# Attention and two gated MLPs on one core: clears, scaling, a mean, a sum and a weight-decoding step stand elsewhere in the order

## The chip, the core and the metric

The kernel runs on one core of a Trainium2 chip. The core has four engines that compute: PE (TensorE, matrix products and transposes), DVE (VectorE), ACT (ScalarE) and POOL (GpSimd). SP (SyncE) issues most of the transfers. Each engine works through its own queue in order; engines wait for one another through semaphores. The metric is the device time of one execution in microseconds (us), lower is better, as the median of three runs.

## What is computed

```python
q_n, k_n = rmsnorm(q, g_q), rmsnorm(k, g_k)          # q, k, v: (4, 12, 448, 64)
scores = (1 / sqrt(64)) * q_n @ k_n.T                # per batch and head
scores = scores - max(scores, axis=-1)
attn = exp(scores)
attn = attn / (sum(attn, axis=-1) + 1e-9)
x = (attn @ v) as (1792, 768)                        # 4*448 tokens, 12*64 features
x = (x @ w_a) * (x @ w_b) @ w_out                    # 768 -> 1536 -> 768
x = sigmoid(x @ w_gate) * (x @ w_val) @ w_out2
```

All of it is fp32. The kernel splits every operand of a large product into a high and a low part and adds three products.

## The kernel before

The work has two stages. **Attention** takes 24 items, an item being two heads of one batch. **The two MLPs** follow as one long stream of matrix products (lines 1026, 1313 and 1323), with weights that are decoded, split and stored on the way.

The order of the attention stage is written out by hand. Four tables hold steps such as `(s, 0, 1)`: `begin` is run once, `first` is the turn for item 1, `turns` is run for each of items 2 to 22, and `end` finishes the last two items and starts the MLPs. In `first` and `turns` the second entry is an offset: in one turn the scores of item i are made, the output of item i-1 is formed, item i-2 is normalised and stored, and items i+1 to i+4 are prepared. What a step issues is put on the engines' queues in the table's order, so the table sets the order on each engine.

The steps that matter here, with their lines:

- `load`, `load_r`, `load_g`: transfers of q, k, the last 64 rows of each head, and the gains g. `load_g` issues its four small transfers from POOL's queue (lines 193, 194); the others come from SP.
- `squares`, `mean` or `sums`, `rsqrt`, `newton`: the factor 1/rms of an item. `mean` (line 251) and `newton` (273 to 275) are on DVE, `rsqrt` (265, 266) on ACT, `squares` of most items on POOL (227 to 229).
- `scale`: q (part 0), k (part 1) and the 64 remaining rows (part 2) times that factor; on DVE for item 0, on POOL for the others (284, 297). `gain` (244) makes the vector G of both gains.
- `t_tr`: PE transposes of the scaled k (part 1) or q (part 0). `k_hi` (339, ACT) and `k_lo` (350, DVE) make the two parts of k, times G; `q_hi` and `q_lo` (334) those of q. The first of k's transposes reads a block that holds the last slot of q and the remaining rows of k.
- `s` (371, PE): scores. `top` (377, DVE): minus their row maximum, nm. `exp` (390, ACT): exponentials P, with row sums. Each item has seven of them; `top` and `exp` of parts 0 and 4 come first in a turn.
- `x_tr` (153, PE) and `x_out` (424 on ACT, 422 on DVE) turn P into pt; `pv` (436, PE) multiplies it with v.
- `rsum` (443, 444, DVE): 1/(sum + 1e-9) of the item before; `rsum_tr`, `rsum_post`, `rsum_get` bring it into rows by PE, ACT and SP; `norm` (473, DVE) multiplies two turns' old output with it; `put` stores.
- `decode(i, 0)` and `decode(i, 1)`: each one step of preparing MLP weights, taken from a generator: it may give DVE one of the lines 721, 723, 727 or 654, ACT one of 720 or 840, a load, or nothing.
- `early_hi` and `early_lo` (499 on ACT, 505 on POOL) split finished outputs in turns 15 to 20. `warm` (533) are transposes on PE whose result nobody reads.

Ahead of `begin` stand memsets: on POOL the identity's, then the tails of three P buffers (line 144), two rs buffers (147) and two rz buffers (156). DVE clears pv and others.

```python
        def rsum(i):
            d = st[i]
            rc = sm.tile([P, 7], F32, tag="rc", name="rc")
            nc.vector.tensor_scalar_add(rc, d["sum"], 1e-9)
            nc.vector.reciprocal(out=rc, in_=rc)
            d["rc"] = rc
```

Of the kernel before, what the change touches and what calls it, by code (L numbers as in the profile page):

```python
# [10 lines left out]
F32 = mybir.dt.float32  # L11
# [3 lines left out]
ALU = mybir.AluOpType  # L15
# [8 lines left out]
def attention_then_two_gated_mlps(  # L24
# [37 lines left out]
    nc = tc.nc  # L62
    B, H, S, D = q.shape
    NT, DM = out.shape
    DFF = moe_w_a.shape[1]
    P = 128
# [48 lines left out]
    def attention():  # L115
        actx = ExitStack()
        pr = actx.enter_context(tc.tile_pool(name="pr", bufs=2))
        sm = actx.enter_context(tc.tile_pool(name="sm", bufs=3))
# [23 lines left out]
        P3 = [fx.tile([P, 512], F32, name=f"P3{i}") for i in range(3)]  # L142
        for t in P3:
            nc.gpsimd.memset(t[:, S:512], 0.0)
        rs = [fx.tile([P, 512], F32, name=f"rs{i}") for i in range(2)]
        for t in rs:
            nc.gpsimd.memset(t, 0.0)
        pvs = ps_v.tile([P, 512], F32, tag="pv", name="pv")
        nc.vector.memset(pvs, 0.0)

        def turned(out, in_, b):
            w = out.shape[-1]
            nc.tensor.transpose(out, in_[rows[b]], ident[rows[b], rows[b]])  # L153
# [8 lines left out]
        st = [dict() for _ in range(NPAIR)]  # L162
# [263 lines left out]
        def pv(i, j):  # L426
# [3 lines left out]
            for h in range(2):  # L430
# [7 lines left out]
                )  # L438

        def rsum(i):  # L440
            d = st[i]
            rc = sm.tile([P, 7], F32, tag="rc", name="rc")
            nc.vector.tensor_scalar_add(rc, d["sum"], 1e-9)
            nc.vector.reciprocal(out=rc, in_=rc)
            d["rc"] = rc

# [83 lines left out]
        def warm(i, n):  # L530
# [4 lines left out]
        begin = (  # L535
            (warm, 0, 26), (load, 0), (load_r0, 0), (load, 1), (load_g, 0), (load_r, -4), (load_r, -3), (load_r, -6),
            (load_r, -5), (load, 2), (load_r, -2), (load_r, -1), (load_v, 0), (squares, 0),
            (sums, 0, (7, 13), (0, 7), (13, 14)), (rsqrt, 0), (squares, 1), (newton, 0),
            (scale, 0, 1), (scale, 0, 2), (gain, 0), (scale, 0, 0), (load, 3), (load_r, 0), (load_v, 1), (load_r, 1),
            (t_tr, 0, 1), (warm, 0, 4), (k_hi, 0), (t_tr, 0, 0), (warm, 0, 6), (sums, 1, (7, 13)), (k_lo, 0), (q_hi, 0),  # L540
# [8 lines left out]

        first = (  # L550
            (mean, 2), (s, 0, 0), (rsqrt, 2), (rsum, -1), (t_tr, 1, 1), (top, 0, 0), (k_hi, 1), (exp, 0, 0), (x_tr, -1, 0), (top, 0, 4),
            (k_lo, 1), (x_out, -1, 0, 0), (s, 0, 1), (x_out, -1, 0, 1), (newton, 2), (exp, 0, 4),
            (x_tr, -1, 1), (x_out, -1, 1, 0), (load, 4), (load_r, 3), (load_v, 1), (t_tr, 1, 0), (rsum_tr, -1), (rsum_post, -1),
            (pv, -1, 0), (scale, 2, 2), (x_out, -1, 1, 1), (top, 0, 1), (q_hi, 1), (scale, 2, 1), (exp, 0, 1), (pv, -1, 1),
            (x_tr, -1, 2), (top, 0, 5), (q_lo, 1), (x_out, -1, 2, 0), (s, 0, 2), (x_tr, -1, 3),
# [3 lines left out]

        turns = (  # L560
            (early, 0), (early_hi, -1), (squares, 3), (early_lo, -1), (decode, 0, 0), (s, 0, 0), (rsum, -1), (t_tr, 1, 1),
            (top, 0, 0), (k_hi, 1), (exp, 0, 0), (x_tr, -1, 0), (top, 0, 4), (k_lo, 1), (x_out, -1, 0, 0), (s, 0, 1),
            (x_out, -1, 0, 1), (norm, -2), (mean, 3), (exp, 0, 4), (x_tr, -1, 1), (x_out, -1, 1, 0),
            (load, 4), (load_r, 3), (load_v, 1), (t_tr, 1, 0), (rsum_tr, -1), (rsum_post, -1), (put, -2),
# [5 lines left out]

        end = (
            (close, -1), (s3, -1, fetch_third, 0), (s, -1, 0), (x_tr, -2, 0), (rsum, -2), (top, -1, 0),
            (exp, -1, 0), (x_out, -2, 0, 0), (top, -1, 4), (x_out, -2, 0, 1), (exp, -1, 4), (norm, -3), (put, -3),
            (x_tr, -2, 1), (s, -1, 1), (x_out, -2, 1, 0), (x_out, -2, 1, 1), (rsum_tr, -2), (rsum_post, -2), (top, -1, 1),
# [3 lines left out]
            (decode, -1, 0), (decode, -1, 1), (x_tr, -1, 0),  # L578
            (close_s, -1), (rsum, -1), (x_out, -1, 0, 0), (decode, -1, 2), (x_out, -1, 0, 1), (x_tr, -1, 1), (rsum_tr, -1), (norm, -2),
            (rsum_post, -1), (put, -2), (x_out, -1, 1, 0), (decode, -1, 3), (x_out, -1, 1, 1), (decode, -1, 4),  # L580
# [821 lines left out]
    with tc.manual_schedule():  # L1402
        main = mlps()
        attention()
        open_places(6, 4, 2, 3)
        begin_mm("mm1", 3)
        for c in range(KC):
            place(where[0]["A22"], "l", c, F32, "f")
        for n, c in (("A22", 0), ("A21", 0), ("A22", 1), ("A21", 1), ("A21", 2), ("A22", 2)):
            stage_in(0, n, c)  # L1410
        for c in range(KC):
            stage_in(0, "A11", c)
        low_third(1)
        sum_third(2)
        next(main)
        cast_third(2)
        next(main)
        next(main)
        low_third(2)
        ready[0] = True  # L1420
        for _ in main:
            pass
# [29 lines left out]
```

## Time and profile before

| | |
|---|---|
| median of three runs | 1211.89 us (1210.01 to 1212.42) |
| the profiled execution's own time | 1213.13 us |
| its span on the core | 1211.4 us |
| PE busy | 1164.7 us, 96% |
| DVE busy | 930.9 us, 77% |
| ACT busy | 666.5 us, 55% |
| POOL busy | 157.3 us, 13% |
| mean granted clock of PE | 0.989 |

The span is read in two parts. Up to about 283 us the four engines share the attention stage, and each of them waits for others; from there PE works without a pause to the end. POOL works in the first part only. Shares over the whole span therefore say little about either part; the stages are read one by one. All times below are from the span's start. "Granted clock" is the share of full speed that PE was given: 1.00 is 2.4 GHz, 0.50 is 1.2 GHz.

### The profile page before, as it was taken

To read this page: it belongs to the slowest core of one execution; us is meant where nothing else is said; L and a number is where in the kernel's file an instruction comes from. 1 tells how busy PE (TensorE), PEld (TensorE's weight loads), DVE (VectorE), ACT (ScalarE), POOL (GpSimd) and SP (SyncE) were. 2 spreads that over 40 slices of the span, in tenths; PEclk is the share of its full clock that TensorE was granted. 3 is DMA by queue.
4 is the path that set the end of the run, shared out by engine and by line. 5 is a ranking of instruction groups with operands and counts; after the bars stand their busy time and mean duration, and the time that the engine had idled before them with its cause. 6 is when DMAs were issued, how large, how long until landed. Compare 5 with 4: busy or idle time off the path is not lost.

```text
span 1211.4 us, 19984 instructions
## 1 busy us (share of the span) xinstructions
PE 1164.7 (96%) x7236; PEld 1009.4 (83%) x7236; DVE 930.9 (77%) x1603; ACT 666.5 (55%) x1298; POOL 157.3 (13%) x246
## 2 busy tenths in 40 slices
PE   6888888999999999999999999999999999999998
PEld 5555554557999999999999999899999999999998
DVE  6899999977868677875768688976776877667673
ACT  5787888974633443444455566544545344445542
POOL 4665577710000000000000000000000000000000
PEclk8999999999999999999999999999999999999999
DMA  5344454439245565654865753234655654777682
GB/s 134 106 132 118 138 155 143 124 107 329 69 134 171 135 210 154 190 185 130 303 232 170 252 168 115 96 110 133 192 188 143 205 169 144 243 274 243 189 272 94
DMA packets 144370, 205.88 MB, mean 170 GB/s; under 512 B 24808, under 2 KB 118160, under 8 KB 144272
## 3 DMA queue, kind: packets, MB, share of 16 engines
q1 hardware_dynamic: 143712, 204.18, 53.9%
q8 instruction: 57, 0.93, 0.3%
q10 hardware_dynamic: 432, 0.43, 0.1%
q14 instruction: 41, 0.34, 0.1%
q0 software_dynamic: 128, 0.00, 0.0%
HBM read 150.21 MB, written 54.35 MB: 169 GB/s over the span
## 4 chain that ended last, share of the span: by engine, by line
PE 82%; DVE 8%; ACT 7%; issue 1%; DMA 1%; POOL 1%; SPq 0%; DVEq 0%; ACTq 0%; POOLq 0%
PE mm L1026 49%; PE mm L1313 13%; PE mm L1323 12%; PE pv L436 4%; ACT P L390 3%; PE s L371 3%; DVE nm L377 2%; ACT pt L424 2%; PE tr L153 2%; DVE pt L422 1%; DVE y L275 1%; DVE xl L654 1%; ACT KH L339 1%; DVE d L727 0%; DMA qk<-in_q_dram 0%
## 5 line engine op out<-in xcount | busy, mean ns | idle before, releaser
L1026 PE MATMUL mm<-xh,wh 128*128 128x448 f32 x1008 | 369.6, 367 | 0.7 <-ACT u L1078 0.4
L1026 PE MATMUL mm<-xh,wl 128*128 128x448 f32 x1008 | 369.0, 366 | 0.8 <-DVE wl L654 0.8
L1026 PE MATMUL mm<-xl,wh 128*128 128x448 f32 x1008 | 368.9, 366 | 0.0
L1026 PEld LDWEIGHTS mm<-xh,wh 128*128 128x128 f32 x1008 | 189.4, 188 | 19.8 <-issue 2.6
L1026 PEld LDWEIGHTS mm<-xh,wl 128*128 128x128 f32 x1008 | 189.5, 188 | 16.9 <-DVE wl L654 1.1
L1026 PEld LDWEIGHTS mm<-xl,wh 128*128 128x128 f32 x1008 | 189.5, 188 | 15.4
L654 DVE TENSOR_TENSOR wl<-d,wh 128x384 fp32r<-128x384 f32 x250 | 136.5, 552 | 66.3 <-ACT wh L1186 41.9
L840 ACT CAST wh<-d 128x384 fp32r<-128x384 f32 x166 | 81.9, 513 | 99.9 <-DVE d L828 80.2
L727 DVE SCALAR_TENSOR_TENSOR d<-d,raw 128x384 uint32<-128x384 uint32 x138 | 77.6, 562 | 53.3 <-ACT d L720 47.8
L390 ACT ACTIVATE P<-s,nm 128x448 f32<-128x448 f32 x166 | 105.3, 642 | 23.1 <-DVE nm L377 23.0
L720 ACT ACTIVATE d<-raw 128x384 f32<-128x384 f32 x138 | 75.9, 555 | 74.9 <-DMA raw<-in_moe_w_out_dram 42.3
L1186 ACT CAST wh<-d 128x384 fp32r<-128x384 f32 x84 | 43.2, 514 | 123.2 <-issue 40.4
L1323 PE MATMUL mm<-wh,gh 128*128 128x384 f32 x294 | 98.7, 336 | 0.2 <-ACT mm L1294 0.2
L1323 PE MATMUL mm<-wl,gh 128*128 128x384 f32 x294 | 98.6, 335 | 0.0
L1323 PE MATMUL mm<-wh,gl 128*128 128x384 f32 x294 | 98.5, 335 | 0.0
L377 DVE TENSOR_REDUCE nm<-s 128x1 f32<-128x448 f32 x166 | 94.0, 612 | 3.3 <-PE s L371 2.6
L1313 PE MATMUL mm<-gh,wl 128*128 128x448 f32 x252 | 92.0, 365 | 0.0
L1313 PE MATMUL mm<-gh,wh 128*128 128x448 f32 x252 | 92.0, 365 | 0.0
L1313 PE MATMUL mm<-gl,wh 128*128 128x448 f32 x252 | 92.0, 365 | 0.0
L371 PE MATMUL s<-KH,QH 64*128 64x448 f32 (+1 forms) x166 | 55.9, 461 | 29.4 <-ACT P L390 29.1
L723 DVE SCALAR_TENSOR_TENSOR raw<-raw 128x384 uint32<-128x384 uint32 x140 | 79.1, 565 | 4.0
L436 PE MATMUL pv<-pt,v 128*64 128x448 f32 x288 | 73.4, 596 | 2.0 <-DVE pt L422 0.6
(162 smaller groups left out, 1924.8 us busy)
## 6 DMA issues: line engine op xcount, KB each, us to landing
gd<-u SPq DMA_DIRECT2D x60, 448.0 KB
u<-gd SPq DMA_DIRECT2D x60, 448.0 KB
d<-wd SPq DMA_DIRECT2D x132, 192.0 KB
raw<-in_moe_w_out_dram SPq DMA_DIRECT2D x48, 384.0 KB
wd<-d SPq DMA_DIRECT2D x72, 192.0 KB
raw<-in_moe_w_a_dram SPq DMA_DIRECT2D x24, 384.0 KB
raw<-in_moe_w_b_dram SPq DMA_DIRECT2D x24, 384.0 KB
raw<-in_moe_w_val_dram SPq DMA_DIRECT2D x23, 384.0 KB
```

Source lines behind the costliest of these rows:

```text
L371: nc.tensor.matmul(out_, w[e, o:o + P], x[e, m:m + S], start=(n == 0), stop=(n == 2))
L377: nc.vector.tensor_reduce(out=d["nm"][:, t:t + 1], in_=d["ps"][t], axis=AX.X, op=ALU.max, negate=True)
L390: nc.scalar.activation(out=e, in_=d["ps"].pop(t), func=AF.Exp, bias=d["nm"][:, t:t + 1], accum_out=d["sum"][:, t:t + 1])
L436: nc.tensor.matmul(pvs[64 * h:64 * h + 64, o:o + S], w, x, start=(n == 0), stop=(n == R), skip_group_check=True)
L654: eng.tensor_tensor(out=lo, in0=t, in1=f32(hi), op=ALU.subtract)
L720: nc.scalar.activation(out=f32(t), in_=f32(high), func=AF.Copy, scale=2.0 ** -112)
L723: nc.vector.scalar_tensor_tensor(out=low, in0=high, scalar=0x80000000, in1=low, op0=ALU.bitwise_and, op1=ALU.bitwise_or)
L727: nc.vector.scalar_tensor_tensor(out=t, in0=t, scalar=3, in1=low, op0=ALU.logical_shift_left, op1=ALU.bitwise_or)
L840: nc.scalar.copy(out=hi, in_=t)
L1026: nc.tensor.matmul(ps[:, o:o + S], w[:, P * c:P * c + P], x[:, x0:x0 + S], start=(p in (1, 5) and c == 0 and z == 0), stop=(c == KC - 1 an ...
L1313: nc.tensor.matmul(ps[:, o:o + S], w[:, P * un:P * un + P], g[:, g0:g0 + S], start=(p in (1, 5) and f == 0 and z == 0), stop=(f == HF - 1 ...
L1323: nc.tensor.matmul(ps[:, o:o + HB], g[:, P * t:P * t + P], w, start=(p in (1, 5) and f == 0 and z == 0), stop=(f == HF - 1 and z == 2), sk ...
```

## The change

- **Prologue.** The clears of the P tails and the rs buffers become a step `clear`, which stands in `begin` behind `load_g`. The rz buffers are still cleared ahead of it.
- **Prologue.** `scale` of item 0: q's scaling follows k's at once; the remaining rows and `gain` come after both.
- **First turn.** `mean` of item 3 (offset 2) moves from the head of `first` to behind the second `x_out`; `rsqrt`, `newton` and `scale` of that item follow later too, and k is scaled ahead of the remaining rows.
- **Sums.** The addition of 1e-9 becomes a step `total` on POOL, ahead of `rsum`. In `turns` it stands behind `squares`, at the turn's head; `rsum` keeps the reciprocal alone and moves from ahead of `top` to behind `norm`. In `first` it moves alike, to behind `mean`. In `end` both stand where `rsum` stood.
- **Decoding.** `decode(0, 0)` moves from the turn's head to behind `norm` and `rsum`.

```diff
-        for t in P3:
-            nc.gpsimd.memset(t[:, S:512], 0.0)
...
-        for t in rs:
-            nc.gpsimd.memset(t, 0.0)
...
+        def clear(i):
+            for t in P3:
+                nc.gpsimd.memset(t[:, S:512], 0.0)
+            for t in rs:
+                nc.gpsimd.memset(t, 0.0)
...
+        def total(i):
+            d = st[i]
+            d["rc"] = sm.tile([P, 7], F32, tag="rc", name="rc")
+            nc.gpsimd.tensor_scalar(out=d["rc"], in0=d["sum"], scalar1=1e-9, scalar2=None, op0=ALU.add)
+
         def rsum(i):
-            d = st[i]
-            rc = sm.tile([P, 7], F32, tag="rc", name="rc")
-            nc.vector.tensor_scalar_add(rc, d["sum"], 1e-9)
+            rc = st[i]["rc"]
             nc.vector.reciprocal(out=rc, in_=rc)
-            d["rc"] = rc
...
-            (early, 0), (early_hi, -1), (squares, 3), (early_lo, -1), (decode, 0, 0), (s, 0, 0), (rsum, -1), (t_tr, 1, 1),
+            (early, 0), (early_hi, -1), (squares, 3), (total, -1), (early_lo, -1), (s, 0, 0), (t_tr, 1, 1),
...
-            (x_out, -1, 0, 1), (norm, -2), (mean, 3), (exp, 0, 4), (x_tr, -1, 1), (x_out, -1, 1, 0),
+            (x_out, -1, 0, 1), (norm, -2), (rsum, -1), (decode, 0, 0), (mean, 3), (exp, 0, 4), (x_tr, -1, 1), (x_out, -1, 1, 0),
```

The order on PE and on SP is the same in both kernels. Three places where it differs follow; the changed kernel's line numbers are up to four higher.

POOL in the prologue, from the identity's memset to the first copy of KH; before:

```order
masks.py:197 MEMSET ident 128x128
L144 MEMSET P_280 128x64
L144 MEMSET P_281 128x64
masks.py:199 ISA
masks.py:199 AFFINE_SELECT ident<-ident 128x128
L144 MEMSET P_282 128x64
L147 MEMSET rs_286 128x512
L147 MEMSET rs_287 128x512
L156 MEMSET rz_292 128x768
L156 MEMSET rz_293 128x768
L193 DMA gg<-in_g_q_dram 64x1
L194 DMA gg<-in_g_k_dram 64x1
```

and in the changed kernel:

```order
masks.py:197 MEMSET ident 128x128
L158 MEMSET rz_287 128x768
masks.py:199 ISA
masks.py:199 AFFINE_SELECT ident<-ident 128x128
L158 MEMSET rz_288 128x768
L195 DMA gg<-in_g_q_dram 64x1
L196 DMA gg<-in_g_k_dram 64x1
L195 DMA gg<-in_g_q_dram 64x1
L196 DMA gg<-in_g_k_dram 64x1
L149 MEMSET P_280 128x64
L149 MEMSET P_281 128x64
L149 MEMSET P_282 128x64
```

Five clears went from ahead of the gain's transfers to behind them, and one clear of rz now stands ahead of the select that makes the identity.

DVE where `begin` ends and the first turn starts (the first nm is still item 0's); before:

```order
L377 TENSOR_REDUCE nm<-s 128x1
L251 TENSOR_REDUCE ms<-sq 128x14
L443 TENSOR_SCALAR rc<-sum 128x7
L444 RECIPROCAL rc<-rc 128x7
L377 TENSOR_REDUCE nm<-s 128x1 x2
L350 SCALAR_TENSOR_TENSOR KL<-tr,G,KH 128x4x64 x2
```

and in the changed kernel:

```order
L379 TENSOR_REDUCE nm<-s 128x1 x3
L352 SCALAR_TENSOR_TENSOR KL<-tr,G,KH 128x4x64 x2
L253 TENSOR_REDUCE ms<-sq 128x14
L449 RECIPROCAL rc<-rc 128x7
L424 COPY pt<-tr 128x7x64
```

The mean and the reciprocal went behind the maxima and k's low part, and the addition left the engine.

DVE from the end of turn 3 into turn 4, with one weight step at each end; before:

```order
L721 TENSOR_SCALAR raw<-raw 128x384
L273 SCALAR_TENSOR_TENSOR t<-y 128x14
L274 SCALAR_TENSOR_TENSOR t<-ms,t 128x14
L275 SCALAR_TENSOR_TENSOR y<-t,y 128x14
L723 SCALAR_TENSOR_TENSOR raw<-raw 128x384
L443 TENSOR_SCALAR rc<-sum 128x7
L444 RECIPROCAL rc<-rc 128x7
L377 TENSOR_REDUCE nm<-s 128x1 x2
L350 SCALAR_TENSOR_TENSOR KL<-tr,G,KH 128x4x64 x2
L473 TENSOR_TENSOR xs<-pv,rs_286 128x512
L251 TENSOR_REDUCE ms<-sq 128x14
L422 COPY pt<-tr 128x7x64
```

and in the changed kernel:

```order
L725 TENSOR_SCALAR raw<-raw 128x384
L275 SCALAR_TENSOR_TENSOR t<-y 128x14
L276 SCALAR_TENSOR_TENSOR t<-ms,t 128x14
L277 SCALAR_TENSOR_TENSOR y<-t,y 128x14
L379 TENSOR_REDUCE nm<-s 128x1 x2
L352 SCALAR_TENSOR_TENSOR KL<-tr,G,KH 128x4x64 x2
L477 TENSOR_TENSOR xs<-pv,rs_283 128x512
L449 RECIPROCAL rc<-rc 128x7
L727 SCALAR_TENSOR_TENSOR raw<-raw 128x384
L253 TENSOR_REDUCE ms<-sq 128x14
L424 COPY pt<-tr 128x7x64
```

The maxima now follow the Newton step directly; the reciprocal and the second weight step stand between `norm` (xs) and `mean` (ms).

## Rows read from the trace of the kernel before

**Rows 1.** Waits of PE, 285 us to the end, longest: us in total, times, longest.
```profile
PE mm L1026 <- DVE wl L654: 0.8, 1, 0.8
```

**Rows 2.** Chain of waits, 0 to 17 us: start us, us, what.
```profile
1.57 0.92 POOL rs L147 x2
...
5.55 3.69 DMA gg<-in_g_k_dram
...
13.87 1.47 PE s L371 x6
```

**Rows 3.** Timeline, prologue: start, us, engine, line, tiles, count [idle before <-releaser].
```profile
8.05 0.27 PE L153 MATMUL tr<-ident,qkn 64*128 64x64 f32 x1 [1.30 <-DVE qkn L297]
...
9.44 0.55 DVE L284 TENSOR_TENSOR qkn<-qk,y 128x384 f32<-128x384 f32 x1
...
10.77 0.69 ACT L339 ACTIVATE KH<-tr,G 128x512 fp32r<-128x512 f32 x1 [3.42 <-PE tr L153]
```

**Rows 4.** Timeline, the first turn's head, several engines.
```profile
25.14 0.47 PE L153 MATMUL tr<-ident,qkn 64*128 64x64 f32 x8 [1.02 <-POOL qkn L297]
...
26.34 1.26 DVE L443 TENSOR_SCALAR rc<-sum 128x7 f32<-128x7 f32 x1
...
28.36 0.64 ACT L390 ACTIVATE P<-s,nm 128x448 f32<-128x448 f32 x1 [0.78 <-DVE nm L377]
...
29.14 0.74 PE L371 MATMUL s<-KH,QH 64*128 64x448 f32 x1 [2.85 <-ACT P L390]
```

**Rows 5.** Timeline of ACT, `k_hi` alone: one for each turn, nine shown.
```profile
40.95 0.69 ACT L339 ACTIVATE KH<-tr,G 128x512 fp32r<-128x512 f32 x1 [0.95 <-PE tr L153]
...
92.38 0.69 ACT L339 ACTIVATE KH<-tr,G 128x512 fp32r<-128x512 f32 x1 [0.54 <-PE tr L153]
104.57 0.69 ACT L339 ACTIVATE KH<-tr,G 128x512 fp32r<-128x512 f32 x1 [0.66 <-PE tr L153]
114.94 0.69 ACT L339 ACTIVATE KH<-tr,G 128x512 fp32r<-128x512 f32 x1 [0.56 <-POOL sq L229]
127.17 0.69 ACT L339 ACTIVATE KH<-tr,G 128x512 fp32r<-128x512 f32 x1 [0.64 <-PE tr L153]
...
199.47 0.69 ACT L339 ACTIVATE KH<-tr,G 128x512 fp32r<-128x512 f32 x1
213.03 0.69 ACT L339 ACTIVATE KH<-tr,G 128x512 fp32r<-128x512 f32 x1
223.03 0.69 ACT L339 ACTIVATE KH<-tr,G 128x512 fp32r<-128x512 f32 x1
...
253.30 0.69 ACT L339 ACTIVATE KH<-tr,G 128x512 fp32r<-128x512 f32 x1 [0.91 <-PE tr L153]
```

**Rows 6.** Timeline of POOL and DVE in the turn from 61 us.
```profile
64.47 0.45 POOL L297 TENSOR_SCALAR qkn<-rqk,y 128x64 f32<-128x64 f32 x1 [3.72 <-PE tr L153]
...
64.78 0.62 DVE L422 COPY pt<-tr 128x448 f32<-128x448 f32 x1 [0.29 <-ACT pt L424]
```

**Rows 7.** Chain of waits, 58 to 125 us, at that turn's head.
```profile
60.79 0.47 DVE raw L723
61.26 0.09 DVE rc L443
...
61.37 0.20 DVE rc L444
```

**Rows 8.** Timeline, POOL and DVE at 199 us.
```profile
199.43 2.07 POOL L505 TENSOR_TENSOR xl<-xst,xh 128x896 fp32r<-128x896 f32 x1 [0.30 <-ACT xh L499]
199.47 2.07 DVE L443 TENSOR_SCALAR rc<-sum 128x7 f32<-128x7 f32 x1
```

**Rows 9.** Timeline of PE and ACT, the turn from 92 us.
```profile
91.31 0.54 ACT L840 CAST wh<-d 128x384 fp32r<-128x384 f32 x1
...
94.52 0.59 PE L371 MATMUL s<-KH,QH 64*128 64x448 f32 x1 [1.54 <-ACT P L390]
```

**Rows 10.** Windows: length, busy of PE, PEld, DVE, ACT, POOL, then PEclk, DMA, GB/s.
```profile
95.00:96.00 1.00, 1.00 (x16) 1.00 (x14) 1.00 (x3) 0.95 (x3) 0.00 (x0) 0.50 0.99 212
```

More of the change, by code (lines that the diff above doesn't have):

```diff
@@ L535, in attention @@
         begin = (
-            (warm, 0, 26), (load, 0), (load_r0, 0), (load, 1), (load_g, 0), (load_r, -4), (load_r, -3), (load_r, -6),
+            (warm, 0, 26), (load, 0), (load_r0, 0), (load, 1), (load_g, 0), (clear, 0), (load_r, -4), (load_r, -3), (load_r, -6),
             (load_r, -5), (load, 2), (load_r, -2), (load_r, -1), (load_v, 0), (squares, 0),
             (sums, 0, (7, 13), (0, 7), (13, 14)), (rsqrt, 0), (squares, 1), (newton, 0),
-            (scale, 0, 1), (scale, 0, 2), (gain, 0), (scale, 0, 0), (load, 3), (load_r, 0), (load_v, 1), (load_r, 1),
+            (scale, 0, 1), (scale, 0, 0), (scale, 0, 2), (gain, 0), (load, 3), (load_r, 0), (load_v, 1), (load_r, 1),
             (t_tr, 0, 1), (warm, 0, 4), (k_hi, 0), (t_tr, 0, 0), (warm, 0, 6), (sums, 1, (7, 13)), (k_lo, 0), (q_hi, 0),
@@ L550, in attention @@
         first = (
-            (mean, 2), (s, 0, 0), (rsqrt, 2), (rsum, -1), (t_tr, 1, 1), (top, 0, 0), (k_hi, 1), (exp, 0, 0), (x_tr, -1, 0), (top, 0, 4),
-            (k_lo, 1), (x_out, -1, 0, 0), (s, 0, 1), (x_out, -1, 0, 1), (newton, 2), (exp, 0, 4),
+            (total, -1), (s, 0, 0), (t_tr, 1, 1), (top, 0, 0), (k_hi, 1), (exp, 0, 0), (x_tr, -1, 0), (top, 0, 4),
+            (k_lo, 1), (x_out, -1, 0, 0), (s, 0, 1), (x_out, -1, 0, 1), (mean, 2), (rsum, -1), (exp, 0, 4),
             (x_tr, -1, 1), (x_out, -1, 1, 0), (load, 4), (load_r, 3), (load_v, 1), (t_tr, 1, 0), (rsum_tr, -1), (rsum_post, -1),
-            (pv, -1, 0), (scale, 2, 2), (x_out, -1, 1, 1), (top, 0, 1), (q_hi, 1), (scale, 2, 1), (exp, 0, 1), (pv, -1, 1),
+            (pv, -1, 0), (rsqrt, 2), (x_out, -1, 1, 1), (top, 0, 1), (q_hi, 1), (newton, 2), (scale, 2, 1), (scale, 2, 2), (exp, 0, 1), (pv, -1, 1),
             (x_tr, -1, 2), (top, 0, 5), (q_lo, 1), (x_out, -1, 2, 0), (s, 0, 2), (x_tr, -1, 3),
@@ L571, in attention @@
         end = (
-            (close, -1), (s3, -1, fetch_third, 0), (s, -1, 0), (x_tr, -2, 0), (rsum, -2), (top, -1, 0),
+            (close, -1), (s3, -1, fetch_third, 0), (s, -1, 0), (x_tr, -2, 0), (total, -2), (rsum, -2), (top, -1, 0),
             (exp, -1, 0), (x_out, -2, 0, 0), (top, -1, 4), (x_out, -2, 0, 1), (exp, -1, 4), (norm, -3), (put, -3),
@@ L578, in attention @@
             (decode, -1, 0), (decode, -1, 1), (x_tr, -1, 0),
-            (close_s, -1), (rsum, -1), (x_out, -1, 0, 0), (decode, -1, 2), (x_out, -1, 0, 1), (x_tr, -1, 1), (rsum_tr, -1), (norm, -2),
+            (close_s, -1), (total, -1), (rsum, -1), (x_out, -1, 0, 0), (decode, -1, 2), (x_out, -1, 0, 1), (x_tr, -1, 1), (rsum_tr, -1), (norm, -2),
             (rsum_post, -1), (put, -2), (x_out, -1, 1, 0), (decode, -1, 3), (x_out, -1, 1, 1), (decode, -1, 4),
```

## The prediction

> **What bounds the kernel now.** I first asked which part of the span can give anything. From 285 us to the end the waits of PE have their longest entry at 0.8 us [rows 1]: the MLP part is PE at work without a pause, and the change touches nothing in it. So a microsecond gained before 283 us is a microsecond at the end, as long as the weights for the first products are ready as early relative to it, and nothing else can be gained. Then I read the attention stage by the moments at which `k_hi` runs, since it runs once a turn [rows 5]. From 40.95 to 253.30 there are 20 distances, 212.35 us together. The shortest kind is 10.0 (213.03 to 223.03): there `k_hi`, the first exponentials and copies on ACT, one copy on DVE, and PE's transposes, scores and pv follow one another around the turn, and the added steps of DVE are not among them. 10.0 us is therefore the floor that an edit on DVE can reach. Three distances are long: 12.19 (from 92.38), 12.23 (from 114.94) and 13.56 (from 199.47). The other 17 sum to 174.37, so 4.37 us above the floor. Third, I read the prologue and the first turn by their chains.
>
> What holds these turns: at a turn's head, the chain runs through DVE, and in front of the maxima stand the weight step (0.47), the addition (0.09) and the reciprocal (0.20) [rows 7]. ACT waits for the first maximum, PE for the exponential. A few microseconds later in the same turn DVE has nothing to do: 0.29 us before its copy of pt [rows 6]. The work stands where it delays, and the gap stands behind it.
>
> At 199 us the cause is another one: the addition, which takes 0.09 on the chain elsewhere, lasts 2.07 us, as long as POOL's L505, which began 0.04 us before it [rows 8]. The same addition lasts 1.26 us in the first turn [rows 4]. In the turn from 92.38 PE waits 1.54 us for the exponential [rows 9] and then has a granted clock of 0.50, that is 1.2 GHz [rows 10].
>
> **The change part by part.**
>
> *Prologue.* The gains' transfers on POOL lose at least the rs clears ahead of them, 0.92 us, so that the last lands at 9.24 - 0.92 = 8.3 us or before [rows 2]. DVE scales q (0.55 us, [rows 3]) in front of the remaining rows instead of behind G. The first transpose, at 8.05, thus moves to 8.6, but needs nothing more after that; before, the others waited until q was scaled at 10.0. Eight transposes end by 9.3 even at the 0.69 us that they took at the low clock, G is ready at about the same moment, and `k_hi` starts at 9.3 instead of 10.77 [rows 3]: 1.5 us. That is the lower end. The upper end, 3.0, holds if PE keeps its full clock: before, it stood idle from 8.3 to 10.0 and then ran six score products in 1.47 us [rows 2], a stretch that the full clock would halve. The clear of rz ahead of the identity delays the `warm` transposes by about half a microsecond, inside PE's idle 1.30 us [rows 3]. The clears that moved run on POOL while it waits for k. I take 2.0, near the lower end, since PE still idles once before the first transpose.
>
> *First turn.* The maxima no longer stand behind the mean and the stretched addition (1.26), so the first exponential follows `k_hi`. `k_hi` no longer waits for the `rsqrt` that needed that mean: the transposes end at 25.14 + 0.47, so `k_hi` ends at 26.3, and the exponential starts then instead of at 28.36 [rows 4]: 2.0 us, the lower end. PE's wait of 2.85 us [rows 4] shrinks to under 1. From that exponential to the next `k_hi` (40.95) it is 12.6 us; a floor turn needs 10.0 less the 0.69 of `k_hi`, so up to 3.3 more could go. I take 1.0 of it, because the mean of item 4, on which ACT waits in this turn, stays where it is. Together 3.0. POOL's scaling starts later by the Newton step's delay, and is needed a turn later.
>
> *Turns 2 to 22.* The addition leaves DVE; reciprocal and weight step go behind `norm`, 0.67 us together where the gap is 0.29 [rows 6, 7], and 0.4 in the floor turns. DVE saves only the 0.09 and what of the gap it fills, so a turn with a weight step there should come to about 10.1 and one without to 10.0. In three turns, two of them the long ones from 92.38 and 114.94, ACT's cast of 0.54 us [rows 9] moves along, from ahead of `k_hi` to between the first copies and the second exponential, where the floor chain passes: they come to 10.4. The 17 ordinary distances keep about 1.5 of their 4.37 us and give 2.9. The two long ones give 12.2 - 10.4 = 1.8 each if PE's wait falls below what it is in the ordinary turns. The third loses the addition's 2.07 and its weight step ahead of `top` and comes to about 10.2: 3.4. Together 9.9.
>
> *The addition on POOL.* No trace shows it there. It is bounded by nothing at all and by POOL's 0.45 us for a tile of 64 columns [rows 6]; I take 0.3. POOL then idles 3.72 us before its next step [rows 6], and DVE's reciprocal comes over 2 us behind it, so it costs nothing in the turns. PE's transpose of the reciprocal now follows it closely, with about 0.1 us to spare. In `end` the reciprocal stands directly behind the addition and ahead of `top`: there it costs 0.3 once on the path.
>
> Sum: 2.0 + 3.0 + 9.9 - 0.3 = 14.6 us. The profiled execution took 1213.13 us in its own time (span 1211.4), so it would become 1198.5; it lies 1.24 above the median, and on the median's scale that is **1197.3**.
>
> **The rivals.**
>
> *POOL holds the moved weight step.* For: DVE instructions do wait for a whole POOL instruction [rows 8], and the moved weight step ends just where POOL starts scaling (64.47, DVE's copy 64.78 in [rows 6]). About 14 turns have one; if it starts second, it waits 0.45 us and pt waits with it: up to 6.3, and half of that when some start first. The time would be 1197.3 + 3 to 6, about 1202. Against: relative to `k_hi` DVE now starts the turn earlier. The Trainium skill, page "SBUF — State Buffer", section "Who interferes with whom", says that a VectorE instruction with two SBUF inputs and a GpSimd instruction that reads SBUF exclude each other, and the second to issue blocks until the first ends. By that rule the weight steps of lines 723, 727 and 654 are of the kind that waits, and the moved addition can make them wait too; the pair at 199 us agrees (2.07 beside 2.07).
>
> *The clock falls as before.* The prologue stays at 1.5, the first turn at 2.0, the two long turns keep their excess: 14.6 - 0.5 - 1.0 - 3.6 = 9.5, so 1202.4. For: PE still waits once a turn. Against: the waits after which it fell (1.54, 2.85) both hang on what moves.
>
> *Nothing arrives at the end.* The attention stage ends earlier, but PE then waits for the first weights: 1211.9. For: the loads hang on the weight steps. Against: these keep their place in each turn, and [rows 1] shows no shortage.
>
> *Slower: more falls of the clock.* The cast, or ACT's part of a weight step, now stands in front of the copy that PE waits for, 0.54 us more in a second wait of the turn. One fall cost 1.8 here. Against a gain of 14.6 with no old fall left, the change turns slower from nine new falls on; in all 14 turns with a weight step it would be 25 - 14.6 = 11 us slower, 1222. Against: turns that had such a cast on ACT already ran at full clock.
>
> **How the numbers follow.** Forecast 0.58, lock 0.16, clock 0.17, nothing arrives 0.05, slower 0.04. The likeliest is 1197.3. Its best end is all upper ends: prologue 3.0, first turn 5.3, turns 11.5, so 1192. The high end takes both losing rivals together, and half of the ordinary turns' gain: 14.6 - 5.1 - 3.1 - 0.4 = 6 us, 1206. About 0.2% (2.4 us) is what a measurement of this kernel can tell from no change. Faster by more than that: 0.91; within it: 0.05; slower: 0.04.
>
> **What would show it.** `k_hi` of item 0 at 9.3 or earlier, and the granted clock at 1.00 there; the first turn's exponential about 4 us earlier than 28.36; `k_hi` distances of 10.0 to 10.4 with none above 11; no idle time of DVE ahead of the turn's first copy of pt; the MLPs starting about 14.6 us sooner. I am wrong if weight steps last 1 us or more behind POOL's scaling, if PE waits for the reciprocal's transpose, if half-clock stretches remain, or if PE waits between the first MLP products.

## The result, and the profile after

The changed kernel takes 1200.76 us (median, 1200.01 to 1203.69) where the kernel before takes 1212.03 us in the same comparison: 11.3 us less, ratio 0.9915 with a 95% interval of 0.9895 to 0.9935. I had predicted 1197.3, in a range of 1192 to 1206. The profiled execution is the slowest of its four, 1203.69 us with a span of 1201.9, so the trace accounts for 9.4 us against the profiled 1213.13 of before.

First the moments of `k_hi`, as in [rows 5]. The timeline of ACT in the changed kernel, `k_hi` (tile KH) and the first turn's first exponential alone; columns are start, duration, engine, line, operation, operands, and in brackets the idle time before it with what ended it.

```profile
9.61 0.69 ACT L341 ACTIVATE KH<-tr,G 128x512 fp32r<-128x512 f32 x1 [1.84 <-DVE G L246]
...
23.74 0.69 ACT L341 ACTIVATE KH<-tr,G 128x512 fp32r<-128x512 f32 x1 [0.40 <-PE tr L155]
24.32 0.63 ACT L392 ACTIVATE P<-s,nm 128x448 f32<-128x448 f32 x1
...
37.78 0.69 ACT L341 ACTIVATE KH<-tr,G 128x512 fp32r<-128x512 f32 x1 [0.94 <-PE tr L155]
...
243.90 0.69 ACT L341 ACTIVATE KH<-tr,G 128x512 fp32r<-128x512 f32 x1 [0.92 <-PE tr L155]
```

The MLP part starts where the chain of waits turns into products alone (start, duration, what). Last row of the chain up to 300 us, changed kernel:

```profile
274.09 26.03 PE mm L1030 x125
```

Before, that start was at 283.47 us by the same view. Behind it PE has no longer wait than the 0.8 us of [rows 1]; its row in the waits of PE from 275 us to the end now reads:

```profile
PE mm L1030 <- DVE wl L658: 0.8, 1, 0.8
```

So all of the gain lies ahead of 274 us, and it can be booked by stretches, each from one marked row to the next:

| stretch | before | after | difference | predicted |
|---|---|---|---|---|
| start to the first turn's exponential | 28.36 | 24.32 | -4.04 | -4.0 |
| from there to the next `k_hi` (40.95, 37.78) | 12.59 | 13.46 | +0.87 | -1.0 |
| 20 distances of `k_hi` (to 253.30, 243.90) | 212.35 | 206.12 | -6.23 | -9.9 |
| last `k_hi` to the MLPs (283.47, 274.09) | 30.17 | 30.19 | 0.0 | +0.3 |
| together | | | -9.4 | -14.6 |

The first row is as predicted. The second and the third are short, by 1.9 and 3.7 us. The 20 distances of after, in order: 10.02, 10.16, 10.25, 10.61, 10.01, 10.61, 10.03, 10.57, 10.01, 10.20, 10.02, 10.17, 10.02, 10.29, 10.47, 10.02, 10.02, **12.18**, 10.46, 10.00. The three long ones of before (12.19, 12.23, 13.56) have become 10.61, 10.57 and 10.02, and a new long one stands at 211 us.

**The new long turn.** The timeline from 201 us, engines together, shows how it comes about (SPq is SP issuing a transfer, in queue order):

```profile
201.24 0.69 ACT L341 ACTIVATE KH<-tr,G 128x512 fp32r<-128x512 f32 x1
...
203.49 0.50 DVE L731 SCALAR_TENSOR_TENSOR d<-d,raw 128x384 uint32<-128x384 uint32 x1
204.02 0.39 SPq L713 DMA_DIRECT2D raw<-in_moe_w_a_dram  x1
204.46 0.48 SPq L204 DMA_DIRECT2D qk<-in_k_dram  x1
205.00 0.46 SPq L204 DMA_DIRECT2D qk<-in_q_dram  x1
...
206.07 0.31 SPq L463 DMA_DIRECT2D dr<-row  x1
...
210.16 1.10 SPq L470 DMA_DIRECT2D rs<-dr  x2
210.32 1.47 POOL L229 TENSOR_TENSOR sq<-qk 128x768 f32<-128x768 f32 x1 [2.55 <-DMA qk<-in_q_dram]
211.26 0.69 ACT L341 ACTIVATE KH<-tr,G 128x512 fp32r<-128x512 f32 x1
213.45 0.25 POOL L445 TENSOR_SCALAR rc<-sum 128x7 f32<-128x7 f32 x1
214.06 0.69 DVE L477 TENSOR_TENSOR xs<-pv,rs 128x512 f32<-128x512 f32 x1 [1.17 <-issue]
214.66 0.19 DVE L449 RECIPROCAL rc<-rc 128x7 f32<-128x7 f32 x1
214.91 0.23 PE L155 MATMUL tr<-ident,rc 64*7 64x64 f32 x2 [0.74 <-DVE rc L449]
```

Read it downwards. The weight step at 203.49 is the one that moved; it is the last reader of a buffer of raw weights, and the next load of raw weights into that buffer stands in SP's queue ahead of k, q and v. The waits of SP from 196 to 216 us name it (total, times, longest):

```profile
SPq L713 <- DVE d L731: 5.1, 1, 5.1
```

Before the change that load went out 0.36 us ahead of this turn's `k_hi` (212.67 against 213.03); now it goes out 2.78 us behind it, with k, q, v and the row of reciprocals behind it in the queue. From the issue of that row to the issue of its broadcast it takes 4.1 us, against 2.5 in the turn before (194.62 to 197.08). POOL's squares wait 2.55 us for q, POOL's addition stands behind the squares, the norm waits 1.17 us for the broadcast (its row names no releaser here; in after_again and more_warm, below, the same wait ends with the broadcast, `rs<-dr`), the reciprocal stands behind the norm and PE waits for it. Then the clock falls to 0.50, that is 1.2 GHz; windows of the changed kernel (columns as in [rows 10]):

```profile
10.00:11.00 1.00, 1.00 (x11) 0.89 (x12) 0.67 (x2) 0.80 (x3) 0.00 (x0) 0.60 0.86 187
...
24.00:30.00 6.00, 5.47 (x40) 3.41 (x38) 4.08 (x10) 4.84 (x14) 3.56 (x6) 0.50 0.38 111
95.00:96.00 1.00, 1.00 (x14) 0.82 (x13) 0.98 (x3) 1.00 (x4) 0.92 (x3) 1.00 0.11 24
215.00:218.00 3.00, 3.00 (x10) 0.71 (x8) 2.53 (x5) 2.27 (x7) 2.83 (x5) 0.50 0.69 229
```

The half-clock stretch of [rows 10] is gone at 95 us, and so are those that stood at 119 to 121 and at 204 to 207 us. The two early ones are there again, somewhat shorter (10 to 13 and 24 to 30 us, before 9 to 16 and 26 to 33), and so is one near the end of the attention stage (266 to 269, before 275 to 278). The one at 215 us is new.

### The profile page after: what moved, and what is told of

The parts are those of the page before. It is cut to its first block, busy times and chain, and to the rows that moved or that the text cites. A ratio compares the mean times of both kernels' runs of the same rounds, so it can differ in the third digit from the quotient of the medians.

```text
span 1201.9 us, 19970 instructions
## 1 busy us (share of the span) xinstructions
PE 1162.0 (97%) x7236; PEld 1007.6 (84%) x7236; DVE 921.9 (77%) x1579; ACT 664.7 (55%) x1298; POOL 163.2 (14%) x270
## 4 chain that ended last, share of the span: by engine, by line
PE 79%; ACT 5%; DVE 5%; POOL 4%; DMA 2%; issue 2%; SPq 2%; POOLq 0%; ACTq 0%; DVEq 0%
PE mm L1030 49%; PE mm L1317 13%; PE mm L1327 12%; PE pv L438 2%; ACT P L392 2%; ACT pt L426 1%; PE s L373 1%; POOL qkn L286 1%; PE tr L155 1%; POOL sq L229 1%; ACT KH L341 1%; POOL sq L231 1%; DMA rqk<-in_k_dram 1%; DVE pt L424 1%; DVE xl L658 1%
```

## Experiments

All times are medians; each is set against the kernel before in its own comparison, since that moved between 1210.84 and 1212.45 from one to the next. Distances of `k_hi` are counted from item 3 on, as in the list above: the 18th is the new long one.

### The four parts alone

**prologue_only**: the kernel before with the new prologue (the clears behind `load_g`, q's scaling ahead of the remaining rows).

```
+ (load_g, 0), (clear, 0), ...
- (scale, 0, 1), (scale, 0, 2), (gain, 0), (scale, 0, 0),
+ (scale, 0, 1), (scale, 0, 0), (scale, 0, 2), (gain, 0),
```

> Theory: the prologue's gain stands by itself and reaches the end: k_hi of item 0 at 9.6 instead of 10.77, the Newton step of item 1 near 14.3 instead of 16.3, and the time 2.0 us under the kernel before (about 1210.0). Rival: the first turn or a later wait takes it back (the transfers of k and q for the next items set the first turn), then the time is within 0.5 us of before. The half-clock stretch from 10 us on should be there in both cases.

Measured: 1209.71 against 1211.88, ratio 0.9983 (0.9974 to 0.9991), 2.2 us less. `k_hi` of item 0 at 9.51. Of the expectation one thing failed: there was no half-clock stretch at 10 us; it came at 18 to 21 us instead. The interval is 1.1 to 3.2 us, and the predicted 2.0 lies in it.

**first_only**: the kernel before with the new first turn.

```
- (mean, 2), (s, 0, 0), (rsqrt, 2), (rsum, -1), (t_tr, 1, 1), ...
+ (total, -1), (s, 0, 0), (t_tr, 1, 1), ...
- (x_out, -1, 0, 1), (newton, 2), ...
+ (x_out, -1, 0, 1), (mean, 2), (rsum, -1), ...
```

> Theory A (what the changed kernel's trace suggests): of the 3.0 us that I predicted only 1.2 arrive, since POOL's addition stands behind the squares of item 4 and PE waits for the reciprocal behind it, and since the clock falls in this turn again: time about 1.2 us under before (1210.8), the distance from k_hi of item 2 to the next k_hi about 14 us. Theory B (the term of my prediction is right and something else in the changed kernel, such as the earlier start, spoils it): 3.0 us under before (1209.0) and that distance near 12.

Measured: 1210.15 against 1211.88, ratio 0.9986 (0.9976 to 0.9997), 1.7 us less (interval 0.4 to 2.9); from `k_hi` of item 2 to the next, 13.33. Between the two theories, nearer to A: the term was sized too high with the change's other parts absent too.

**sums_only**: the kernel before, with the addition on POOL and the reciprocal behind the norm, in the turns and at the end; the weight step stays at the head.

```
- (squares, 3), (early_lo, -1), (decode, 0, 0), (s, 0, 0), (rsum, -1), (t_tr, 1, 1),
+ (squares, 3), (total, -1), (early_lo, -1), (decode, 0, 0), (s, 0, 0), (t_tr, 1, 1),
- (norm, -2), (mean, 3)
+ (norm, -2), (rsum, -1), (mean, 3)
```

> Only the +1e-9 on POOL and the reciprocal behind the norm, in the turns and at the end; weight step, first turn and prologue as before. The stretched addition at 199 us is gone, and 0.29 us leave the head of each turn: 3 to 5 us under before, about 1208. On the long turn at 211 us of the changed kernel: theory S (SP: the weight step that moved carries the next raw weight load with it, and the loads of k and q queue behind that) expects no long turn here, all of the last eight distances of k_hi at 10.6 or less. Theory R (the reciprocal now hangs on the norm, which hangs on the broadcast of the turn before, and this ring has too little room) expects one here too, of 11.5 us or more, with an idle of DVE ahead of the norm.

Measured: 1202.70 against 1211.88, ratio 0.9924 (0.9912 to 0.9936), 9.2 us less, twice what I expected. The 20 distances sum to 203.61, less than in the changed kernel (206.12), and the 18th is 10.22: no long turn. Turns with a weight step at their head take 10.00 to 10.20, apart from the two old long ones (10.65 and 10.66), and those without one 10.18 to 10.30 from the tenth on. So the 0.47 us of the weight step in front of the maxima [rows 7] are almost fully hidden once the 0.29 us of addition and reciprocal are gone. Of the 8.74 us that the distances lost, 3.43 are the turn at 199 us and 3.11 the two old long turns, and a good part of these three is clock that did not fall here (see "The two old long turns" below); the other 17 turns gave 2.2.

**decode_only**: the kernel before with only the weight step behind the norm.

```
- (decode, 0, 0), (s, 0, 0), (rsum, -1), ...    (norm, -2), (mean, 3)
+ (s, 0, 0), (rsum, -1), ...    (norm, -2), (decode, 0, 0), (mean, 3)
```

> Only the weight step behind the norm, the rest as before. It frees 0.47 us at the head of 14 turns, but three turns keep the cast of 0.54 us on the way: 3 to 4 us under before, about 1208.5. Theory S expects SP to wait some 5 us ahead of one raw load in the turn that the stretched addition had made long (near 210 us), and k's load to start about 3 us after that turn's k_hi, instead of 0.4 us before it; whether the turn then becomes long tells if the late load is enough or needs the reciprocal behind the norm as well. Theory R expects k's load no later than before, and no long turn.

Measured: 1206.74 against 1211.88, ratio 0.9954 (0.9941 to 0.9966), 5.1 us less, more than expected. The 20 distances sum to 206.18, as in the changed kernel (206.12). In the profiled execution the first turn, which this edit doesn't touch, took 16.41 us with the clock at half for most of it, so single turns of one execution say little here. Here too SP waits for the moved step, from 192 to 225 us:

```profile
SPq L709 <- DVE d L727: 5.5, 1, 5.5
```

and k's load starts at 210.32, 3.25 us behind its turn's `k_hi` (207.07), as theory S had it. The 18th distance is 10.55 and the 19th 10.78, where sums_only has 10.22 and 10.04: the late load costs something here as well, but makes no long turn. Of the 0.74 in the 19th, about 0.4 is ACT's part of the weight step (see old_decode). In this kernel the reciprocal does not stand behind the norm; that this is why the turn stays short is not shown.

The four gains sum to 18.2 us, and the change that holds all four gains 11.3. The prologue and the first turn come early and don't overlap with the rest, so the sums (9.2) and the weight step (5.1) gain in part the same time: both take the addition away from POOL's long instruction [rows 8] (in decode_only it runs at 196.20 us for 0.16, ahead of that instruction at 197.02), where prologue_only and first_only, which leave it, have turns of 14.75 and 14.86, each with a half-clock stretch of over 6 us.

### The weight step, its load and the reciprocal

**old_decode**: the changed kernel with the weight step back at the head of the turn.

```
- (total, -1), (early_lo, -1), (s, 0, 0), ...    (rsum, -1), (decode, 0, 0), (mean, 3)
+ (total, -1), (early_lo, -1), (decode, 0, 0), (s, 0, 0), ...    (rsum, -1), (mean, 3)
```

> The changed kernel with the weight step back at the head of the turn; prologue, first turn and sums stay. Theory S (the moved weight step costs more than it gives, by the late raw load): the sum of the parts measured alone, 2.2 + 1.7 + 9.2 = 13.1 us under before, about 1198.8, some 2 us faster than the changed kernel; no distance of k_hi above 10.7. Rival (the parts are worth less together, since each of them cured the same falls of the clock): equal to the changed kernel or slower, 1200.8 or above.

Measured: 1198.25 against 1212.45, ratio 0.9888 (0.9872 to 0.9904), 14.2 us less. The sum of the parts is there (13.1), and this kernel is faster than the changed one by its median, though the two intervals overlap. The traces are clearer: with the step moved, the 20 distances sum to 203.78 to 206.70 (the changed kernel, after_again, late_raw, recip_first, more_warm); with it at the head and the sums moved, to 203.46 to 203.65 (old_decode, with 203.53, sums_only, dve_add, total_early, mean_early). The moved weight step loses, it doesn't gain. Turn by turn, the moved step gains about 0.1 us in most turns with one (10.02 against 10.12), but in three turns loses 0.42 to 0.44 (10.61, 10.47 and 10.46 against 10.19, 10.03 and 10.04), and 1.95 in the 18th.

In these three, ACT's part of the weight step moved along. The timeline of ACT in the changed kernel from 69 us shows one of them, a cast, between the first copies and the second exponential:

```profile
69.45 0.96 ACT L426 COPY pt<-tr 128x448 f32<-128x448 f32 x2
70.29 0.54 ACT L844 CAST wh<-d 128x384 fp32r<-128x384 f32 x1
70.70 0.66 ACT L392 ACTIVATE P<-s,nm 128x448 f32<-128x448 f32 x1
```

**late_raw**: the changed kernel with the load of raw weights in that one turn issued behind k, q and v; all engines keep their order.

```
-            fill()
+            if late:
+                late.append(fill)
+            else:
+                fill()
...
+            if i == 18:
+                late.append(None)
...
- (load_v, 1), (t_tr, 1, 0)
+ (load_v, 1), (fill_late, 0), (t_tr, 1, 0)
```

> The changed kernel with one transfer moved: in the turn of item 18 the raw weight load is issued behind the loads of k, q and v of that turn, instead of ahead of them; every engine keeps its order. Theory S: k's load starts about 3 us earlier against that turn's k_hi, POOL's squares no longer wait 2.5 us for q, the turn of 12.18 us becomes 10.0 to 10.4 and the one behind it 10.0; time 2.0 to 2.5 us under the changed kernel, about 1198.5. Theory R (the ring over norm and reciprocal has too little room whatever the loads do): the turn stays at 11.5 or more.

Measured: 1199.90 against 1212.45, ratio 0.9902 (0.9886 to 0.9919). The timeline of SP around that turn:

```profile
197.52 0.39 SPq L204 DMA_DIRECT2D qk<-in_k_dram  x1
202.40 0.37 SPq L721 DMA_DIRECT2D raw<-in_moe_w_a_dram  x1
203.01 0.29 SPq L463 DMA_DIRECT2D dr<-row  x1
```

k's load starts 2.1 us ahead of the turn's `k_hi` (199.61), the norm of the next turn waits for nothing, and the 18th distance is 10.02 (209.63 to 219.65). The engines that compute keep their order, so the load's place in SP's queue makes the wait. The other traces agree: the 18th distance is 10.55 to 12.82 in the five with the late load (the changed kernel, after_again, recip_first, more_warm, decode_only) and 10.02 to 10.24 in the nine with the load ahead. How much of the excess is wait and how much clock is told under after_again. By time, the gain over the changed kernel (1.6 us by the ratios) is inside the intervals.

**recip_first**: the changed kernel with the reciprocal ahead of the norm.

```
- (norm, -2), (rsum, -1), (decode, 0, 0)
+ (rsum, -1), (norm, -2), (decode, 0, 0)
```

> The changed kernel with the reciprocal ahead of the norm, so that it no longer waits for the broadcast of the turn before. Theory S with the ring as its carrier: SP still waits 5 us for the moved weight step and the norm is still about 1 us late in that turn, but PE no longer waits for the reciprocal, and the turn comes to 10.7 or less; about 1 to 2 us under the changed kernel. If the late k and q alone make the turn long, it stays near 12. Rest of the turns unchanged within 0.1 us.

Measured: 1200.41 against 1212.45, ratio 0.9899 (0.9882 to 0.9915). SP waits 5.3 us for the moved step, the 18th distance is 10.67. But the ring was not the only carrier, as the timelines of DVE and PE show: the reciprocal no longer waits for the norm, it waits for POOL's addition, which stands behind the late squares; and PE now waits for the late norm itself, which reads the pv that PE writes next.

```profile
210.88 0.20 DVE L449 RECIPROCAL rc<-rc 128x7 f32<-128x7 f32 x1 [0.64 <-POOL rc L445]
211.42 0.69 DVE L477 TENSOR_TENSOR xs<-pv,rs 128x512 f32<-128x512 f32 x1 [0.33 <-DMA rs<-dr]
212.17 2.03 PE L438 MATMUL pv<-pt,v 128*64 128x448 f32 x8 [0.58 <-DVE xs L477]
```

**after_again**: the changed kernel itself once more.

> The changed kernel once more, for a second look at what varies between executions. Theory: the late raw load is in the program, so SP waits about 5 us for the moved weight step again, the norm of the next turn comes about 1 us late and that turn takes about 10.7; the other 1.5 us of the 12.18 came from the fall of the clock, which need not come again. The time is that of the result, 1200.8 within 1 us. Rival: the whole 12 us come again, clock fall and all, or the turn is 10.0 and the late load was an accident of one execution.

Measured: 1201.06 against 1210.84, ratio 0.9923 (0.9909 to 0.9936). SP waits 4.6 us for the moved step. The timeline of DVE shows the norm late again:

```profile
213.89 0.69 DVE L477 TENSOR_TENSOR xs<-pv,rs 128x512 f32<-128x512 f32 x1 [1.76 <-DMA rs<-dr]
```

The 18th distance is 12.82, with a half-clock stretch from 215 to 218 us again: the rival is right that it recurs. In recip_first and more_warm, with the same late load, the clock did not fall there, and the turn took 10.67 and 10.69. PE's waits in that turn are the same in both, as its timelines show. The changed kernel, where the clock then fell:

```profile
212.62 0.47 PE L373 MATMUL s<-KH,QH 64*128 64x448 f32 x1 [0.76 <-ACT P L392]
```

with 0.74 us more at 214.91 (above); and more_warm, where it did not:

```profile
211.80 0.47 PE L373 MATMUL s<-KH,QH 64*128 64x448 f32 x1 [0.76 <-ACT P L392]
214.04 0.22 PE L155 MATMUL tr<-ident,rc 64*7 64x64 f32 x2 [0.69 <-DVE rc L449]
```

So of the 2 to 3 us that this turn takes above its neighbours about 0.65 are the waits (0.6 more in after_again, where PE waits 1.33 us for the reciprocal), and 1.5 the clock, which fell behind them in two of the five executions with the late load. That the waits bring the fall is not shown; in the nine executions without them it did not fall there.

### Place or engine

**dve_add**: old_decode, but the addition on DVE, right ahead of the reciprocal, behind the norm.

```
- nc.gpsimd.tensor_scalar(out=d["rc"], in0=d["sum"], scalar1=1e-9, scalar2=None, op0=ALU.add)
+ nc.vector.tensor_scalar_add(d["rc"], d["sum"], 1e-9)
...
- (squares, 3), (total, -1), (early_lo, -1) ...    (norm, -2), (rsum, -1)
+ (squares, 3), (early_lo, -1) ...    (norm, -2), (total, -1), (rsum, -1)
```

> The kernel with the weight step at its old place (old_decode, 1198.25), but the +1e-9 back on DVE, right ahead of the reciprocal and behind the norm: the place of the change without its engine. Theory P (the gain of the sums comes from their place): within 0.7 us of old_decode, turns of 10.0 to 10.2, and in the first turn PE waits less for the reciprocal. Theory E (the engine counts: on DVE the addition meets POOL's long instructions again and is held, as the 2.07 us at 199 us were): one or more stretched additions of 0.5 us or more on the way, 1 to 3 us slower than old_decode.

Measured: 1197.37 against 1210.84, ratio 0.9893 (0.9880 to 0.9905). That is faster than both kernels; the changed kernel has 0.9923 (0.9909 to 0.9936) in the same comparison, 3.7 us more. The group of the addition, all 24 of them (duration in ns, least, median, most):

```profile
L445 DVE TENSOR_SCALAR rc<-sum x24: 154/156/662, 25.2 to 258.6; 128x7 f32<-128x7 f32 x24
```

Against old_decode, the ratios are 0.9893 and 0.9888 and the 20 distances sum to 203.54 and 203.53: no difference. So theory P: the place away from the head makes the gain, and POOL isn't needed for it. One addition was stretched, to 0.66 us in the first turn, where the one at the head was held for 2.07 [rows 8]; it made nothing slower that the time or the distances show.

### The first turn

**more_warm**: the changed kernel with more idle transposes, (warm, 0, 34) for 26 in the prologue, and (warm, 0, 7) ahead of `t_tr` in the first turn.

> The changed kernel with 8 more idle transposes in the prologue and 7 at the head of the first turn, which write nothing that is read. Theory C (PE's idle time ahead of the first transposes, 1.57 us in the prologue and 0.98 us in the first turn, is what the clock falls after): no stretch of 0.50 at 10 to 13 us, nor at 24 to 30; the first turn falls from 14.0 to about 12.5 and the time to 2 us under the changed kernel. Rival (the clock falls for another reason, or the turn's length comes from the waits on POOL and the mean): both stretches stay, and the time is within 0.7 us of the changed kernel.

Measured: 1200.55 against 1212.45, ratio 0.9906 (0.9891 to 0.9921). No stretch of 0.50 at 10 to 13 us, but neither has any of the three kernels compared beside it, with no more transposes. In the first turn the clock fell at 27.2 us instead of 23.8, and the turn took 14.04, as in the changed kernel. That is nearer the rival, of which one part failed: the early stretch did not stay, it came at 17 to 20 us. That the added transposes do anything for the clock is not shown.

**total_early**: old_decode with POOL's first addition ahead of the squares of item 4.

```
- (load_r, 3), (squares, 4),                 first: (total, -1), (s, 0, 0)
+ (load_r, 3), (total, 0), (squares, 4),     first: (s, 0, 0)
```

> The kernel with the weight step at its old place, and POOL's first addition ahead of the squares of item 4 instead of behind them. Theory W (PE's wait for the reciprocal of up to 1.2 us and the rsqrt behind it make the first turn): the first turn falls from 12.84 to 13.0 to about 12.0 where the clock stays up. Rival (DVE's row of Newton steps, QL, copy and mean behind it sets the turn): 12.7 to 13.0 as before, and the time within 0.3 us of old_decode.

Measured: 1199.35 against 1210.84, ratio 0.9908 (0.9895 to 0.9920). PE's wait for the reciprocal (1.2 us in after_again and recip_first) is gone, and the mean of item 4 runs 6.49 us behind the turn's `k_hi` instead of 7.25 in recip_first, where the clock was full up to there as well. But the clock fell in this turn from 30 to 34 us, and it took 13.65. Neither theory can be judged by the turn's length.

**mean_early**: total_early, and the mean of item 4 ahead of DVE's copy of pt.

```
- (q_lo, 1), (x_out, -1, 2, 0) ...   (mean, 3), (rsqrt, 3)
+ (q_lo, 1), (mean, 3), (x_out, -1, 2, 0) ...   (rsqrt, 3)
```

> As total_early, and in the first turn the mean of item 4 ahead of DVE's copy of pt, in an idle stretch of DVE, so that the rsqrt that ACT waits 3 us for comes about 1.1 us sooner. If that rsqrt is what holds the turn, the first turn loses another 0.6 us, to 11.5 to 12.3 with the clock up, and the time is 0.5 to 1.5 us under old_decode, the fastest of all, about 1197.3. Rival: the scores or the copies of pt are late next, nothing changes beyond 0.3 us.

Measured: 1198.66 against 1210.84, ratio 0.9898 (0.9883 to 0.9912). The timeline of its first turn, `k_hi`, addition, reciprocal, mean and `rsqrt` alone:

```profile
22.85 0.69 ACT L341 ACTIVATE KH<-tr,G 128x512 fp32r<-128x512 f32 x1 [0.22 <-PE tr L155]
23.26 0.25 POOL L445 TENSOR_SCALAR rc<-sum 128x7 f32<-128x7 f32 x1
...
25.43 0.19 DVE L449 RECIPROCAL rc<-rc 128x7 f32<-128x7 f32 x1
...
28.82 0.61 DVE L253 TENSOR_REDUCE ms<-sq 128x14 f32<-128x448 f32 x1
29.46 0.31 ACT L267 ACTIVATE y<-ms,eps 128x14 f32<-128x14 f32 x1 [1.43 <-DVE ms L253]
...
34.34 0.69 ACT L341 ACTIVATE KH<-tr,G 128x512 fp32r<-128x512 f32 x1 [0.95 <-PE tr L155]
```

The turn takes 11.49, the only one under 12. recip_first is the other kernel with full clock through this turn, and has 12.84: 1.35 us from the two moved rows at equal clock, by one execution of each. At the end of the attention stage the clock fell for longer than elsewhere in this execution (0.50 from 260 to 266 us), so from the last `k_hi` to the MLPs it took 31.67 us, against 30.19 in the changed kernel with its shorter fall there and 28.73 in old_decode with none. So the gain in the first turn doesn't show in this execution's time, and the ratio (0.9898, against 0.9888 of old_decode) doesn't show it either: the expected fastest time of all did not come. No run joins these two moves with dve_add.

## Why the forecast was 3.5 us too low

**The prologue (2.0 predicted).** 2.2 measured alone, and in the trace the Newton step of item 1 is 2.0 us earlier. The way there was another one: `k_hi` at 9.61 instead of 9.3, and a half-clock stretch of 3 us instead of none at 10 us. Kernels with the same prologue have `k_hi` at 8.94 to 9.61.

**The first turn (3.0 predicted).** The 2.0 for the head arrived exactly: the exponential comes 4.04 us earlier, 2.0 of it from the prologue. The further 1.0 did not; the rest of the turn became 0.87 us longer. The mis-sized term is "I take 1.0 of it", which came out as 0.87 us lost. I had named the mean of item 4 as what stays, but not that the addition, now on POOL, would stand behind 3.1 us of squares in this turn. The timeline of the changed kernel:

```profile
24.14 1.47 POOL L229 TENSOR_TENSOR sq<-qk 128x768 f32<-128x768 f32 x1
...
26.05 1.14 POOL L231 TENSOR_TENSOR sq<-sq 128x448 f32<-128x448 f32 x1
27.27 0.25 POOL L445 TENSOR_SCALAR rc<-sum 128x7 f32<-128x7 f32 x1
27.56 0.20 DVE L449 RECIPROCAL rc<-rc 128x7 f32<-128x7 f32 x1 [1.15 <-POOL rc L445]
```

And the clock fell here again (24 to 30 us). Alone the first turn's edit measured 1.7.

**The turns (9.9 predicted, 6.2 in the trace).** By the prediction's own groups: the two long turns gave 3.24 (predicted 3.6), the third 3.54 (3.4). The 17 ordinary ones were to give 2.9 and lost 0.55. Three terms are in that:

- The late load: 1.94 us in the 18th distance. The step that failed is the sentence on the loads, "these keep their place in each turn". It was argued for the end of the stage only; that the moved step carries a load in SP's queue, and that k, q, v and the row stand behind it, I had not followed in any single turn. In the other turns with such a load, it goes out ahead of `k_hi`.
- ACT's parts of the weight step. I had counted three casts, 10.4 each. Five turns have an ACT part there, and take 10.46 to 10.61. Two of the five are the old long turns, which have 10.64 and 10.65 with the step at its old place as well; in the other three 1.03 us are lost against before.
- The weight step was given the larger share of the head's 0.76 us. sums_only shows the opposite: without the 0.29 of addition and reciprocal the turns fall from 10.45 to 10.13, and the 0.47 that remain cost about 0.1. The turns without a weight step at their head fell as well, the tenth and the twelfth from 10.45 to 10.18 each.

**The two old long turns.** Their excess is 0.5 to 0.6 us of work and 1.3 of fallen clock, and the fall is not part of the program: prologue_only and first_only leave these turns as they were, and have 12.24 and 10.92, and 10.93 and 10.94. The prediction counted on curing a fall that comes in some executions.

**The third long turn.** It came to 10.02, as forecast (10.2). What held it was more than the addition of [rows 8]; the weight step just ahead of it was held too, as DVE's timeline of the kernel before shows:

```profile
198.03 1.51 DVE L723 SCALAR_TENSOR_TENSOR raw<-raw 128x384 uint32<-128x384 uint32 x1
```

With the 2.07 that is 3.58 us, as much as the whole excess over 10.0; the clock also stood at half from 204 to 207 us of that turn, which the prediction didn't name. How the two share the excess is not shown.

**The end and the addition.** POOL's addition takes 0.25 us (0.3 taken). The 0.3 at the end didn't show.

**The rivals.** That POOL would hold the moved weight steps did not come true: the steps of lines 725, 727 and 731 last at most 0.80 us in the whole program. It is the old place that is held: in old_decode four steps last 1.31 to 1.52 us beside POOL's squares, and yet their turns take 10.03 to 10.11, so the holding costs next to nothing there. The timeline of old_decode shows one of the four:

```profile
196.97 1.17 POOL L231 TENSOR_TENSOR sq<-sq 128x448 f32<-128x448 f32 x1
197.05 1.52 DVE L731 SCALAR_TENSOR_TENSOR d<-d,raw 128x384 uint32<-128x384 uint32 x1
198.24 0.43 POOL L445 TENSOR_SCALAR rc<-sum 128x7 f32<-128x7 f32 x1
```

The rule that I quoted from the Trainium skill, page "SBUF — State Buffer", section "Who interferes with whom", is in line with this pair: the step has two SBUF inputs (d and raw), and it ends 0.43 us after POOL's squares. The pair at 199 us, which the prediction set beside that rule, is not of its kind, as the addition reads one tile; it shows the holding, but not the rule as quoted.

That the clock would fall as before came half true: in the prologue and the first turn yes, in the two long turns no. The rival on the slower side had its place right (ACT's part in front of the copy, 0.42 to 0.44 us in three turns), but no fall followed there. The cost of a fall was put at 1.8 us; the pairs of turns above give 1.3 and 1.5.

**The signs and the range.** Of the forecast's own signs the exponential came (4.04 us earlier) and no weight step lasted 1 us. The others failed: `k_hi` of item 0 at 9.61, a distance of 12.18, the MLPs 9.4 us sooner instead of 14.6, PE waiting 0.74 us for the reciprocal, and half-clock stretches left. That the time still lies well inside the range is in part luck: the sums, of which I expected the smaller share, carry the turns, and cover what the moved weight step loses (206.12 against 203.53). The range's upper end also doesn't add up as worded: half of the ordinary turns' 2.9 is 1.45, not 0.4, which would make it 1207.

What stays open: why the clock falls behind a wait in one execution and not in the next, and so what any one edit is worth within about 1.5 us a place.

## What to carry to other kernels

A step that is moved takes its transfers with it: list for every turn what it issues, what stands behind that in the queue, and who waits for that, before the step is called free. Of several steps in front of a wait only as much counts as lies above the next-longest chain, so try each alone; here the smallest ones gave 9.2 us, and the largest, which gave 5.1 alone, lost beside them. And a small step belongs where nobody waits for it at once, whichever engine does it: a step that POOL held for 1 us cost next to nothing where there was slack behind it.

## What the runs showed of the hardware

- The granted clock falls to 0.50 in different places from one execution of a program to the next: in the changed kernel at 10 to 13 and 24 to 30 us in one, and at 17 to 20 and 27 to 30 in the other, with 215 to 218 and 266 to 269 in both. Behind PE waits of 0.76 and 0.74 us it fell, behind 0.76 and 0.69 us at the same place in a sister kernel it stayed up.
- In the changed kernel a transfer of 3.5 KB, issued 0.5 us behind the last of 960 KB of loads, had its follower issued 4.1 us later, and SP waited 1.1 of them for it to land (1.9 in after_again). In the kernel before, in the same turn, it was issued 2.2 us behind the same loads, its follower came 2.1 us later, and SP's waits list none for it.
- An addition on 128x7 takes 0.25 us on POOL and 0.16 on DVE in these kernels.
